# A RetNet block and a SiLU block on one core: the k and q scalings on VectorE instead of GpSimd, and the masks ahead of x and the state

## The chip, the cores and the metric

The kernel runs on one core of a Trainium2 chip. A core has TensorE (PE in the profile; PEld is its loading of weights), VectorE (DVE), ScalarE (ACT), GpSimd (POOL) and SyncE (SP), which here only issues transfers. Each engine takes its own instructions in order, and waits for others through semaphores. The metric is the device time of one execution in microseconds (us).

## The reference

Two blocks follow each other. The first is a recurrent linear attention with a decay for each of the 8 heads, over 4 batches, 768 positions and a head width of 64. The second is a pair of products with a SiLU gate between them, 512 to 2048 to 512, over the 3072 tokens of the first.

```python
for t in range(S):
    state = gamma[None, :, None, None] * state + np.einsum('bhd,bhe->bhde', k[:, :, t], v[:, :, t])
    y[:, :, t] = scale * np.einsum('bhd,bhde->bhe', q[:, :, t], state)
...
h = x @ w_in
g = h * (1.0 / (1.0 + np.exp(-h)))
return (g @ w_out).astype(np.float32)
```

x is y with heads and batches laid out as tokens.

## The kernel before

**Units and visits.** The 768 positions are cut into 6 chunks of 128. A unit is one chunk of one batch, so there are 24, in the order chunk 0 of batches 0 to 3, chunk 1 of batches 0 to 3, and so on. `visit()` (L356) number m works on three units at once: `stage_t(m)` (L274) transposes k and q of unit m on TensorE, and ScalarE copies them out of PSUM; `stage_y(m-2)` (L299) makes the new part of the state (L309) and the output y from the old state (L318) and from the masked scores (L323); `stage_a(m-1)` (L284) makes the scores of unit m-1 (L290), and VectorE multiplies them by the decay mask (L296, "am"). After that the next k, q and v are asked for, and `scale_k(m-1)` and `scale_q(m-1)` run on GpSimd (L266, L272): k is multiplied by one number per position and head, and the transposed q by one per position. Both are done in place. They follow the transposition and the scores, which need the unscaled values; the scaled ones are used by L309 and L318 in the next visit. k is not scaled in the last chunk and q not in the first, so there are 20 scalings of each. When a unit of batch 0 comes, `next_chunk()` (L248) first moves the factors of q (gq) on by one chunk, also on GpSimd (L249).

**x and the state.** Within `stage_y`, y goes from its PSUM bank into x, as three parts that TensorE can multiply: ScalarE writes the first (L339), VectorE the second from y and the first (L340) and the third from the second (L341). The new part of the state is added to the old on VectorE (L335), or copied by ScalarE in chunk 0 (L333). For chunk 2 (`LATE`), y goes to DRAM (L328, L329) and is split later.

**Banks.** One visit asks for six PSUM banks of a pool of four: k transposed, q transposed, the new part of the state, y, and the two halves of the scores. A bank is free again when what is in it has been read: by ScalarE for the transposes, by L335 (or L333) for the state, by L339 and L340 for y, by L296 for the scores.

**The first product.** `product_in(c, f)` (L376) is 12 matmuls over 128x512 (L383 to L385) for one of 16 columns of w_in, with two PSUM results, and ScalarE, VectorE and ScalarE after it (L387, L388, L389). `take_w()` (L186) brings the next piece of the weights to float32 and cuts it into three parts: six VectorE instructions in `convert_w` (L168 to L180) and, for w_in, two more in `split_w` (L105, L108), with ScalarE steps between them (L166, L103, L107).

**Order.** Visits 0 to 5 run back to back, with takes after visits 0, 1, 3 and 4. Then come the first half of the columns of chunk 0, with a visit after most single products and a take beside nearly all; the first half of chunk 1 with three visits; then the second halves of both without visits. From chunk 2 on there is a visit after every fourth product and, until the last chunk, a take at every third. Then the second product runs for all chunks (L502 to L504). TensorE's order is as written. On every other engine a planner sets the order when the kernel is built: it goes by the order of the program and by when, by its own reckoning, an instruction can start.

Of the kernel before, what the change touches and what calls it, by code (L numbers as in the profile page):

```python
# [16 lines left out]
ALU = mybir.AluOpType  # L17
# [14 lines left out]
def kernel(  # L32
# [24 lines left out]
    nc = tc.nc  # L57
# [3 lines left out]
    NC = S // C  # L61
# [51 lines left out]
    units = [(c, b) for c in range(NC) for b in range(B)]  # L113
    kqv = {"k": {}, "q": {}, "v": {}}

    def load(name, n):
        if n >= len(units):
            return
        c, b = units[n]
        src = {"k": k, "q": q, "v": v}[name]  # L120
        t = ld.tile([128, H, D], FP32, tag=f"{name}f", name=f"{name}f_{n}",
                    bufs=4 if name == "k" else 2)
        nc.sync.dma_start(out=t, in_=src[b, :, ds(c * C, C)].rearrange("h t d -> t h d"))
        kqv[name][n] = t
# [98 lines left out]
    gq = const.tile([128, HP, C], FP32, tag="gq", name="gq")  # L223
# [24 lines left out]
    def next_chunk():  # L248
        nc.gpsimd.tensor_tensor(out=gq, in0=gq,  # L249
                                in1=step[:, :HP].unsqueeze(2).to_broadcast([128, HP, C]),  # L250
                                op=ALU.mult)
# [2 lines left out]
             for b in range(B)]  # L254


    xt, kt, qt, am = {}, {}, {}, {}

    def bank(name):
        return ps_a.tile([128, 512], FP32, tag="a", name=name)  # L260

    def scale_k(n):
        if 0 <= n < len(units) and units[n][0] < NC - 1:
            t = kqv["k"][n]
            g = gk[:, units[n][0], :].unsqueeze(2).to_broadcast([128, H, D])
            nc.gpsimd.tensor_tensor(out=t, in0=t, in1=g, op=ALU.mult)  # L266

    def scale_q(n):
        if 0 <= n < len(units) and units[n][0] > 0:
            if units[n][1] == 0:  # L270
                next_chunk()
            nc.gpsimd.tensor_tensor(out=qt[n], in0=qt[n], in1=gq, op=ALU.mult)  # L272

    def stage_t(n):  # L274

        for name, src, to, bufs in (("k", kqv["k"][n], kt, 2), ("q", kqv["q"].pop(n), qt, 3)):
            tp = bank(f"{name}tp_{n}").rearrange("p (a t) -> p a t", a=HP)
            for a in range(HP):
                nc.tensor.transpose(tp[:, a, :], src[:, 2 * a : 2 * a + 2, :], ident)  # L279
            t = one.tile([128, HP, C], FP32, tag=f"{name}t", name=f"{name}t_{n}", bufs=bufs)  # L280
            evac[:] = [nc.scalar.copy(out=t, in_=tp).ins]
            to[n] = t

    def stage_a(n):  # L284

        ap = [bank(f"sc{j}_{n}").rearrange("p (a t) -> p a t", a=HP) for j in range(2)]
        ktn = kt.pop(n)
        for a in range(HP):
            for j in range(2):
                nc.tensor.matmul(ap[j][:, a, :], lhsT=ktn[ts(j, D), a, :],  # L290
                                 rhs=qt[n][ts(j, D), a, :], start=True, stop=True,
                                 skip_group_check=True)
        am[n] = []
        for j in range(2):
            t = one.tile([128, HP, C], FP32, tag=f"am{j}", name=f"am{j}_{n}")
            nc.vector.tensor_tensor(out=t, in0=ap[j], in1=decay[:, j], op=ALU.mult)  # L296
            am[n].append(t)

    def stage_y(n):  # L299

        c, b = units[n]
        kf, vs = kqv["k"].pop(n), kqv["v"].pop(n)
        qtn, amn = qt.pop(n), am.pop(n)
        if c < NC - 1:
            sp = bank(f"s_{n}")[:, : HP * D].rearrange("p (a e) -> p a e", a=HP)
            for a in range(HP):
                for j in range(2):
                    h = 2 * a + j
                    nc.tensor.matmul(sp[ts(j, D), a, :], lhsT=kf[:, h, :], rhs=vs[:, h, :],  # L309
                                     start=True, stop=True, skip_group_check=True)  # L310
        if b == 0 and c != LATE:
            xt[c] = xpool.tile([128, 3, KIN, NT], FP32R, tag="xt", name=f"xt_{c}")
        yp = bank(f"y_{n}").rearrange("p (a t) -> p a t", a=HP)

        if c > 0:
            for a in range(HP):
                for j in range(2):
                    nc.tensor.matmul(yp[ts(j, D), a, :], lhsT=state[b][ts(j, D), a, :],  # L318
                                     rhs=qtn[ts(j, D), a, :], start=(a == 0), stop=False,
                                     skip_group_check=True)  # L320
        for a in range(HP):
            for j in range(2):
                nc.tensor.matmul(yp[ts(j, D), a, :], lhsT=vs[:, 2 * a + j, :],  # L323
                                 rhs=amn[j][:, a, :], start=(c == 0 and a == 0), stop=True,
                                 skip_group_check=True)
        if c == LATE:
            y = hpool.tile([128, KIN, C], FP32, tag="hs", name=f"ys_{b}")
            nc.scalar.copy(out=y, in_=yp)  # L328
            nc.sync.dma_start(out=y_dram[b], in_=y)  # L329
        else:  # L330
            split_x(c, b, yp)
        if c == 0:
            nc.scalar.copy(out=state[b], in_=sp)  # L333
        elif c < NC - 1:
            nc.vector.tensor_tensor(out=state[b], in0=state[b], in1=sp, op=ALU.add)  # L335

    def split_x(c, b, y):
        xh, xl, xm = (xt[c][:, i, :, ts(b, C)] for i in range(3))
        nc.scalar.activation(out=xh, in_=y, func=AF.Copy, scale=HALF)  # L339
        nc.vector.tensor_tensor(out=xl, in0=y, in1=xh.bitcast(FP32), op=ALU.subtract)  # L340
        nc.vector.scalar_tensor_tensor(out=xm, in0=xl.bitcast(FP32), scalar=-1.0 / EPS,  # L341
                                       in1=xh.bitcast(FP32), op0=ALU.mult, op1=ALU.add)
# [13 lines left out]
    def visit():  # L356
        m = visits[0]
        visits[0] += 1
        if m - 2 >= len(units):
            return  # L360
        if m < len(units):
            stage_t(m)
        if m >= 2:
            stage_y(m - 2)
        if 1 <= m <= len(units):
            stage_a(m - 1)
        load("k", m + 2)
        load("q", m + 2)
        load("v", m)
        scale_k(m - 1)  # L370
        scale_q(m - 1)


    pending = []
# [64 lines left out]

    ctx.enter_context(tc.manual_schedule(engines={mybir.EngineType.PE}))  # L440
    take_w(visit)
    chunk_decays()
    for m in range(1, B + 2):
        visit()
        if m in (1, 3, 4):
            take_w()
        if m == 2:
            first_chunk()
# [5 lines left out]
    for c, f0, at, takes in phases:  # L454
        for i in range(half):
            product_in(c, f0 + i)
            if i in takes:
                take_w()
            put_g(1)
            if i in at:  # L460
                visit()
            if (c, f0) == (1, half) and 1 <= i <= B:
                late_x(i - 1)
# [22 lines left out]
    for c in range(NC):  # L486
# [7 lines left out]
        for f in range(NF):  # L494
            n = c * NF + f
            split(n + S_AHEAD)
            t = ready.pop(n)
# [44 lines left out]
```

## Time and profile before

| | before |
|---|---|
| median of 3 runs | 679.35 us (679.28 to 680.01) |
| the profiled execution | 680.86 us |
| its span in the profile | 679.1 us |
| TensorE busy | 646.3 us |
| VectorE busy | 432.0 us, 680 instructions |
| ScalarE busy | 282.0 us |
| GpSimd busy | 60.1 us, 84 instructions |

The span runs from the first to the last instruction in the profile; the time of the execution has 1.76 us around it. A busy share is an average over stages that have different limits: the stages before 150 us, with the visits and takes close together, and the long rest have to be read apart. An instruction's duration holds the time that it was kept from running on its engine; the idle time before it is shown beside it, with what ended it.

### The profile page before, as it was taken

The page shows a single profiled execution, that of the slowest core. Times are in us where ns is not written, and L with a number is a line of the kernel's source. Part 1 is how long each engine was busy: PE and PEld are TensorE (multiplying, and loading weights), DVE is VectorE, ACT ScalarE, POOL GpSimd, SP SyncE. Part 2 cuts the span into 40 slices and gives each one's busy share as a digit, 9 for nine tenths or more (in the row PEclk, how much of TensorE's full clock was granted, in tenths as well). Part 3 has the DMA queues.
Part 4 walks back from the last instruction along what each step waited for, and adds up shares of the span by engine and source line. Part 5 has one row for each costly group of instructions (what it writes and reads, how often), then busy time and mean ns, then how long its engine had stood idle before and what let it go on. Part 6 is the DMA issues. An engine that isn't in the chain of part 4 may idle for free.

```text
span 679.1 us, 10363 instructions
## 1 busy us (share of the span) xinstructions
PE 646.3 (95%) x3904; PEld 529.7 (78%) x3904; DVE 432.0 (64%) x680; ACT 282.0 (42%) x510; POOL 60.1 (9%) x84
## 2 busy tenths in 40 slices
PE   5778889999999999999999999999999999999997
PEld 3567777767888888878888888888888888888885
DVE  4899999995557675867444876545455463644641
ACT  6455466454544454443435885122222232321311
POOL 5123312300011211011000000000000000000000
PEclk9889999999999999999999999999999999999999
DMA  9958767766456665766322774424253252523401
GB/s 223 204 104 194 177 174 216 203 214 217 140 169 178 189 208 164 218 195 202 110 77 93 224 202 150 125 96 153 82 167 95 98 175 67 174 78 121 145 11 63
DMA packets 122546, 103.45 MB, mean 152 GB/s; under 512 B 79488, under 2 KB 87680, under 8 KB 122496
## 3 DMA queue, kind: packets, MB, share of 16 engines
q1 hardware_dynamic: 119040, 96.49, 50.1%
q10 hardware_dynamic: 3456, 6.29, 2.5%
q8 instruction: 31, 0.51, 0.3%
q14 instruction: 19, 0.16, 0.1%
HBM read 66.06 MB, written 36.70 MB: 151 GB/s over the span
## 4 chain that ended last, share of the span: by engine, by line
PE 82%; DVE 11%; DMA 2%; ACT 2%; issue 1%; SPq 1%; DVEq 0%; ACTq 0%
PE oa L503 13%; PE ob L504 13%; PE oa L502 13%; PE ha L383 11%; PE hb L385 11%; PE ha L384 11%; PE y L323 3%; PE sc L290 2%; PE y L318 2%; DVE wi L108 1%; DVE am L296 1%; PE qtp L279 1%; PE s L309 1%; DVE cs L173 1%; DVE wil L105 1%; DVE cs L180 1%
## 5 line engine op out<-in xcount | busy, mean ns | idle before, releaser
L385 PE MATMUL hb<-xt,wi 128*128 128x512 f32 x384 | 150.5, 392 | 4.9 <-DVE g L388 3.1
L383 PE MATMUL ha<-xt,wi 128*128 128x512 f32 x384 | 152.1, 396 | 0.0
L384 PE MATMUL ha<-xt,wi 128*128 128x512 f32 x384 | 149.8, 390 | 0.0
L504 PE MATMUL ob<-wo,gs 128*128 128x512 f32 x384 | 149.6, 390 | 0.0
L502 PE MATMUL oa<-wo,gs 128*128 128x512 f32 x384 | 149.4, 389 | 0.0
L503 PE MATMUL oa<-wo,gs 128*128 128x512 f32 x384 | 149.4, 389 | 0.0
L430 DVE TENSOR_TENSOR gs<-gr,gs 128x512 fp32r<-128x512 f32 x96 | 62.4, 685 | 92.6 <-ACT gs L428 92.6
L428 ACT ACTIVATE gs<-gr 128x512 fp32r<-128x512 f32 x96 | 53.4, 620 | 140.2 <-issue 129.7
L388 DVE TENSOR_TENSOR g<-g,hb 128x512 f32<-128x512 f32 x96 | 65.6, 684 | 69.4 <-ACT g L387 68.8
L385 PEld LDWEIGHTS hb<-xt,wi 128*128 128x128 f32 x384 | 72.1, 188 | 23.1 <-DVE g L388 6.1
L389 ACT ACTIVATE g<-g 128x512 f32<-128x512 f32 x96 | 60.6, 631 | 61.6 <-DVE g L388 61.6
L383 PEld LDWEIGHTS ha<-xt,wi 128*128 128x128 f32 x384 | 72.1, 188 | 17.4 <-ACT g L387 0.7
L504 PEld LDWEIGHTS ob<-wo,gs 128*128 128x128 f32 x384 | 72.1, 188 | 15.9 <-DVE o L510 1.1
L503 PEld LDWEIGHTS oa<-wo,gs 128*128 128x128 f32 x384 | 72.1, 188 | 15.0
L502 PEld LDWEIGHTS oa<-wo,gs 128*128 128x128 f32 x384 | 72.1, 188 | 14.9 <-ACT o L509 0.2
L384 PEld LDWEIGHTS ha<-xt,wi 128*128 128x128 f32 x384 | 72.1, 188 | 14.5 <-DVE xt L340 0.2
L387 ACT ACTIVATE g<-ha 128x512 f32<-128x512 f32 x96 | 56.7, 591 | 59.5 <-PE ha L384 54.8
L431 DVE SCALAR_TENSOR_TENSOR gs<-gs 128x512 fp32r<-128x512 f32 x96 | 62.3, 684 | 0.4
L510 DVE TENSOR_TENSOR o<-o,ob 128x512 f32<-128x512 f32 x24 | 15.9, 686 | 39.2 <-ACT o L509 39.2
L272 POOL TENSOR_TENSOR qt<-qt,gq 128x512 f32<-128x512 f32 x20 | 27.4, 1369 | 128.4 <-PE sc L290 96.2
L509 ACT ACTIVATE o<-oa 128x512 f32<-128x512 f32 x24 | 13.7, 597 | 56.7 <-PE oa L503 49.1
L266 POOL TENSOR_TENSOR kf<-kf,gk 128x512 f32<-128x512 f32 x20 | 22.7, 1134 | 154.4 <-PE ktp L279 146.2
(59 smaller groups left out, 606.8 us busy)
## 6 DMA issues: line engine op xcount, KB each, us to landing
gd<-g SPq DMA_DIRECT2D x96, 256.0 KB, 3.0
gr<-gd SPq DMA_DIRECT2D x96, 256.0 KB, 2.7
wf<-in_moe_w_in_dram SPq DMA_DIRECT2D x16, 512.0 KB, 4.2
wf<-in_moe_w_out_dram SPq DMA_DIRECT2D x16, 512.0 KB, 3.5
kf<-in_k_dram SPq DMA_DIRECT2D x24, 256.0 KB, 4.6
qf<-in_q_dram SPq DMA_DIRECT2D x24, 256.0 KB, 4.8
vf<-in_v_dram SPq DMA_DIRECT2D x24, 256.0 KB, 4.2
out_dram<-o ACTq DMA_DIRECT2D x24, 256.0 KB, 2.1
```

Of the source, the lines that this page charges most:

```text
L383: nc.tensor.matmul(ha, lhsT=w[0], rhs=x[0], start=first_, stop=False)
L384: nc.tensor.matmul(ha, lhsT=w[1], rhs=x[1], start=False, stop=last)
L385: nc.tensor.matmul(hb, lhsT=w[2], rhs=x[2], start=first_, stop=last)
L387: nc.scalar.activation(out=hs, in_=ha, func=AF.Copy, scale=ONE_E)
L388: nc.vector.tensor_tensor(out=hs, in0=hs, in1=hb, op=ALU.subtract)
L389: nc.scalar.activation(out=hs, in_=hs, func=AF.Silu)
L428: nc.scalar.activation(out=t[:, 0, :], in_=g, func=AF.Copy, scale=HALF)
L430: nc.vector.tensor_tensor(out=t[:, 1, :], in0=g, in1=high, op=ALU.subtract)
L431: nc.vector.scalar_tensor_tensor(out=t[:, 2, :], in0=t[:, 1, :].bitcast(FP32), scalar=-1.0 / EPS, in1=high, op0=ALU.mult, op1=ALU.add)
L502: nc.tensor.matmul(oa, lhsT=gh, rhs=wo[f][:, 0, :], start=first_, stop=False)
L503: nc.tensor.matmul(oa, lhsT=glo, rhs=wo[f][:, 1, :], start=False, stop=last)
L504: nc.tensor.matmul(ob, lhsT=gm, rhs=wo[f][:, 2, :], start=first_, stop=last)
```

## The change

Both scalings are issued on VectorE. `next_chunk()` stays on GpSimd. The part of `stage_y` that follows its matmuls (y into x, the state) becomes `finish_y`, which keeps the two PSUM tiles in `live` until it runs. In a visit the scalings now stand right behind `stage_a`, q before k, and `finish_y(m-2)` behind them; the three loads come last. The matmuls keep their order, and the store of y in `finish_y` still stands ahead of the visit's loads.

```diff
     def scale_k(n):
         if 0 <= n < len(units) and units[n][0] < NC - 1:
             t = kqv["k"][n]
             g = gk[:, units[n][0], :].unsqueeze(2).to_broadcast([128, H, D])
-            nc.gpsimd.tensor_tensor(out=t, in0=t, in1=g, op=ALU.mult)
+            nc.vector.tensor_tensor(out=t, in0=t, in1=g, op=ALU.mult)
...
             if units[n][1] == 0:
                 next_chunk()
-            nc.gpsimd.tensor_tensor(out=qt[n], in0=qt[n], in1=gq, op=ALU.mult)
+            nc.vector.tensor_tensor(out=qt[n], in0=qt[n], in1=gq, op=ALU.mult)
...
+        live[n] = sp if c < NC - 1 else None, yp
+
+    def finish_y(n):
+        c, b = units[n]
+        sp, yp = live.pop(n)
         if c == LATE:
...
             stage_y(m - 2)
         if 1 <= m <= len(units):
             stage_a(m - 1)
+            scale_q(m - 1)
+            scale_k(m - 1)
+        if m >= 2:
+            finish_y(m - 2)
         load("k", m + 2)
         load("q", m + 2)
         load("v", m)
-        scale_k(m - 1)
-        scale_q(m - 1)
```

More of the change, by code (lines that the diff above doesn't have):

```diff
@@ L254 @@
              for b in range(B)]
-    xt, kt, qt, am = {}, {}, {}, {}
+    xt, kt, qt, am, live = {}, {}, {}, {}, {}
     def bank(name):
```

## The prediction

> **What bounds the kernel now.** I read the page first, then the busy times by stage, then who waits for whom in the early stages, then single rows.
>
> ```profile
> span 679.1 us, 10363 instructions
> PE 646.3 (95%) x3904; PEld 529.7 (78%) x3904; DVE 432.0 (64%) x680; ACT 282.0 (42%) x510; POOL 60.1 (9%) x84
> ...
> 14.00:41.00 27.00, 19.52 (x221) 15.84 (x221) 23.90 (x36) 12.47 (x26) 5.71 (x6) 0.87 0.86 168
> 41.00:85.00 44.00, 37.73 (x376) 30.89 (x373) 42.97 (x65) 21.43 (x38) 13.36 (x10) 1.00 0.75 174
> 85.00:147.00 62.00, 56.93 (x439) 45.58 (x438) 59.72 (x98) 35.20 (x63) 11.44 (x9) 1.00 0.73 197
> 147.00:360.00 213.00, 211.96 (x1443) 174.20 (x1442) 131.62 (x205) 97.25 (x168) 23.25 (x19) 1.00 0.55 173
> ```
>
> The last four rows are stages: limits, length, then busy time of PE, PEld, DVE, ACT and POOL, the granted clock, the DMA share and GB/s. Over the whole span TensorE is the bound. From 147 us on it is idle for 213.00 - 211.96 = 1.04 us up to 360, where the last scaling has run: nothing that VectorE saves or loses there shows, as long as it is not late. From 14 to 147 us it is otherwise. VectorE is busy 42.97 of 44 and 59.72 of 62 us, which is 102.7 of 106, and 23.90 of 27 before that; TensorE has 7.48 + 6.27 + 5.07 = 18.8 us idle there. Only these can be won. The waits of the first stage (two rows) and of 41 to 147 us (three rows) say for whom it waits:
>
> ```profile
> PE qtp L279 <- DVE xt L340: 4.7, 2, 2.3
> PE y L323 <- DVE am L296: 1.1, 2, 0.9
> ...
> PE s L309 <- DVE am L296: 4.5, 2, 2.5
> PE hb L385 <- DVE g L388: 2.1, 3, 1.0
> PE hb L385 <- DVE xt L341: 1.8, 1, 1.8
> ```
>
> All are VectorE: its backlog sets how fast TensorE gets through this part, and the end comes when TensorE has done what is left. So the question is what the change does to VectorE's work before 147 us.
>
> **What it removes.** One scaling of k beside VectorE's instructions, in order of time:
>
> ```profile
> 28.18 0.68 DVE L177 SCALAR_TENSOR_TENSOR cp<-wf,cp 128x512 f32<-128x512 uint32 x1
> 28.66 1.11 POOL L266 TENSOR_TENSOR kf<-kf,gk 128x512 f32<-128x512 f32 x1 [6.33 <-PE ktp L279]
> 28.78 1.53 DVE L341 SCALAR_TENSOR_TENSOR xt<-xt 128x512 fp32r<-128x512 f32 x1
> 30.24 1.28 DVE L296 TENSOR_TENSOR am<-sc,decay 128x512 f32<-128x512 f32 x2
> ```
>
> GpSimd begins at 28.66 us and ends at 29.77. L341, begun behind it, takes 1.53 us; an instruction of its kind and size beside it takes 0.68. It looks as if L341 does its work once GpSimd has ended. By the Trainium skill, "SBUF — State Buffer", section "Who interferes with whom", a VectorE instruction with two SBUF inputs, or one in a two-port mode, and a GpSimd instruction that reads SBUF exclude each other for a whole instruction; the two rows agree, and by that rule the whole lengthening goes. How often it happens, from VectorE's groups in 41 to 147 us (seven rows) and in 137 to 160 us, where GpSimd does nothing (four rows):
>
> ```profile
> L108 DVE SCALAR_TENSOR_TENSOR wi<-wi,wil 128x512 fp32r<-128x512 f32 x13 | 12.3, 942 | 0.2
> L173 DVE SCALAR_TENSOR_TENSOR cs<-ca,cs 128x512 uint32<-128x512 uint32 x14 | 12.0, 861 | 0.3
> L105 DVE SCALAR_TENSOR_TENSOR wil<-cs,wi 128x512 f32<-128x512 f32 x13 | 10.4, 801 | 1.9 <-ACT wi L103 1.5
> L180 DVE TENSOR_TENSOR cs<-cs,cp 128x512 f32<-128x512 f32 x12 | 10.0, 831 | 0.1
> L170 DVE TENSOR_SCALAR ca<-ca 128x512 f32<-128x512 f32 x13 | 9.3, 717 | 0.0
> L175 DVE TENSOR_SCALAR cp<-cs 128x512 uint32<-128x512 uint32 x14 | 7.1, 509 | 0.2
> L341 DVE SCALAR_TENSOR_TENSOR xt<-xt 128x512 fp32r<-128x512 f32 x5 | 4.5, 893 | 0.0
> ...
> L173 DVE SCALAR_TENSOR_TENSOR cs<-ca,cs 128x512 uint32<-128x512 uint32 x4 | 2.8, 692 | 0.1
> L180 DVE TENSOR_TENSOR cw<-cs,cp 128x512 f32<-128x512 f32 x4 | 2.8, 692 | 0.3 <-DMA wod<-cw 0.2
> L170 DVE TENSOR_SCALAR ca<-ca 128x512 f32<-128x512 f32 x4 | 1.7, 423 | 1.0 <-ACT ca L166 1.0
> L175 DVE TENSOR_SCALAR cp<-cs 128x512 uint32<-128x512 uint32 x4 | 1.7, 423 | 0.1
> ```
>
> Against 692 ns for the two-tensor forms and 423 for L170 and L175, the excess is 13 x 0.250 (L108) + 14 x 0.169 (L173) + 13 x 0.109 (L105) + 12 x 0.139 (L180) + 13 x 0.294 (L170) + 14 x 0.086 (L175) + 5 x 0.201 (L341) = 14.7 us. In 14 to 41 us, three groups are long by the same measure:
>
> ```profile
> L173 DVE SCALAR_TENSOR_TENSOR cs<-ca,cs 128x512 uint32<-128x512 uint32 x3 | 3.5, 1172 | 0.1
> L341 DVE SCALAR_TENSOR_TENSOR xt<-xt 128x512 fp32r<-128x512 f32 x3 | 2.9, 960 | 0.0
> L168 DVE TENSOR_SCALAR cs<-wf 128x512 uint32<-128x512 uint32 x2 | 1.7, 841 | 0.0
> ```
>
> 3 x 0.480 + 3 x 0.268 + 2 x 0.418 = 3.1 us. Who makes it, from GpSimd's groups in 14 to 147 us and one of its gq steps beside L180:
>
> ```profile
> L266 POOL TENSOR_TENSOR kf<-kf,gk 128x512 f32<-128x512 f32 x12 | 14.2, 1179 | 48.1 <-PE ktp L279 39.9 <-issue 8.2
> L272 POOL TENSOR_TENSOR qt<-qt,gq 128x512 f32<-128x512 f32 x9 | 13.1, 1458 | 40.3 <-PE sc L290 31.4 <-ACT wi L103 6.2 <-ACT xt L339 2.7
> L249 POOL TENSOR_TENSOR gq<-gq,step 128x512 f32<-128x512 f32 x3 | 3.2, 1083 | 0.8 <-ACT gq L246 0.6
> ...
> 122.10 1.10 POOL L249 TENSOR_TENSOR gq<-gq,step 128x512 f32<-128x512 f32 x1
> ...
> 122.23 1.52 DVE L180 TENSOR_TENSOR cs<-cs,cp 128x512 f32<-128x512 f32 x1
> ```
>
> Twelve scalings of k (four before 41 us) and nine of q go; the three gq steps stay, and one of them costs L180 1.52 - 0.69 = 0.83 us. For the three I leave 1.1 us in place (bounds: nothing, or 3 x 0.83 = 2.5). Removed: 14.7 + 3.1 - 1.1 = 16.7 us, or 0.80 for each of 21.
>
> **What it adds.** 21 VectorE instructions of 128x512 with three f32 operands in SBUF, as L180 is (692 ns). What one takes from VectorE is the step to the next instruction:
>
> ```profile
> 41.08 0.69 DVE L340 TENSOR_TENSOR xt<-y,xt 128x512 fp32r<-128x512 f32 x1 [0.55 <-ACT xt L339]
> 41.69 0.68 DVE L105 SCALAR_TENSOR_TENSOR wil<-cs,wi 128x512 f32<-128x512 f32 x1
> 41.70 1.79 POOL L272 TENSOR_TENSOR qt<-qt,gq 128x512 f32<-128x512 f32 x1 [6.24 <-ACT wi L103]
> 42.29 1.75 DVE L341 SCALAR_TENSOR_TENSOR xt<-xt 128x512 fp32r<-128x512 f32 x1
> ...
> 44.09 0.50 PE L385 MATMUL hb<-xt,wi 128*128 128x512 f32 x1 [1.77 <-DVE xt L341]
> ```
>
> 41.08 to 41.69 to 42.29: 0.60 us each. The trace has no VectorE instruction whose input is broadcast as gk is; its step is bounded by 0.42 (the whole of a one-tensor L170 undisturbed) and 0.73 (0.69 and a small gap). I take 0.60, the nearest row: 21 x 0.60 = 12.6 us, between 8.8 and 15.3.
>
> **The sum.** Before 41 us four scalings: 4 x 0.60 - 3.1 = -0.7. From 41 to 147 us seventeen: 17 x 0.60 = 10.2, less 14.7 - 1.1 = 13.6, so -3.4. Together -4.1 us of VectorE's work, between -7.9 and -1.4 with the bounds of the added step. VectorE has next to no idle time there, so I pass it on whole. The profiled execution was 680.86 us for a span of 679.1: it would become 676.8, its span 675.0. It lies 1.5 us over the median of 679.35, from which I get 675.25, rounded to **675.2 us**.
>
> **Moves costed at nothing.** The scalings issue no transfer; y's store (L329) and the loads keep their order on SP's queue. In 147 to 360 us the added steps lie beside a TensorE that has its inputs ready. The masks now come before L340 and L341: x is up to four steps (2.4 us) later, but VectorE does the same work, and a stall of 0.7 to 0.9 us per scaling is gone. A scaling of q for batch 0 waits for gq on GpSimd, and behind it in VectorE's queue stand the scaling of k, x, the state and the next take. GpSimd has nothing else to do and can start gq once the last scaling of the chunk before is done, a whole visit ahead. If it did not, each of five would cost 1.1 us, and only two fall into 41 to 147 us: 2.2.
>
> **Rivals.**
> *The order pays too* (chance 0.15). The masks free two score banks first, and the two transposes of the next visit can go there instead of waiting for L340 (4.7 us), and L309 no longer for L296 (4.5). While VectorE is the bound, this can win only its idle time, 27 - 23.90 + 106 - 102.7 = 6.4 us. All of it gives 668.8; I put the case at half, 672.0. Against it: VectorE's idle time is partly waits for ScalarE inside a take.
> *The saving is not passed on* (0.14). TensorE is itself busy 94.7 of 106 us. If VectorE's free time turns into waits for TensorE or ScalarE, half of it or less arrives at the end: 677.3 to 679.4, which I put at 678.6.
> *The banks of y and of the state are held longer* (0.11): slower. They are now freed behind two masks and two scalings. TensorE waits for them if its next visit asks for a third bank before VectorE is through, and between visits 6 to 10 it has one product of 12 matmuls, at 0.23 us each 2.8, to cover four steps of 0.60 and L340, 3.0. If every visit up to 85 us lost its scalings, that is 4 x 0.60 in chunk 0 and 5 x 1.20 after it, 8.4 us, and the first product, which already waits 1.77 us for L341 at 44.09, would lose 2.4 more. With the saving: 675.2 + 10.8 = 686.0; with only half of the visits hit, 680.6. I put it at 683. For it: TensorE's waits for L340. Against it: the rows at 41.08 and 41.69, where VectorE takes L340 before the masks because it is ready first; the planner may do so again.
> *The lengthening has another cause, and VectorE just gets more work* (0.03): 679.35 + 12.6 = 692.0. The Trainium skill, "Perfetto Trace Analysis", section "Optimizing Scalar/DVE Operations", says that with a saturated VectorE some work may go to GpSimd, which speaks against this change; it adds that the two share a port, so that it might not help. Against the rival: L341 above, and that VectorE's long rows lie beside GpSimd's.
> That the planner puts the scalings or x elsewhere than written is part of the forecast, since the sum doesn't hang on the order.
>
> **How the numbers follow.** The forecast has 0.57, with its own range from 671.4 (-7.9) to 677.9 (-1.4). A measurement can tell about 0.2%, 1.4 us: faster is below 678.0. Faster: 0.57 + 0.15 = 0.72; same: 0.14; slower: 0.11 + 0.03 = 0.14. The range of 8 in 10 reaches down to 670.5, into the first rival, and up to 681.0, over the second and the lower part of the third.
>
> **What would show it.** Right: VectorE's long rows are at 692 and 423 ns in 41 to 147 us but for those beside L249; L266 and L272 on VectorE at about 0.69 us; VectorE's busy time about as before (it counts 0.69 for a step of 0.60); TensorE's idle time in 14 to 147 us near 14.7 us instead of 18.8. Wrong: scalings at 1 us and more, long rows that stay, waits of L309 or L323 for L340, L333 or L335 that add up to over 4 us, or any new idle time of TensorE after 147 us.

## The result and the profile after

| | before | after |
|---|---|---|
| median of 4 runs on one chip | 679.68 us (679.28 to 680.19) | 663.60 us (662.50 to 663.89) |
| ratio, 95% interval | | 0.976 (0.9743 to 0.9777) |
| the profiled execution and its span | 680.86, 679.1 us | 663.32, 661.2 us |

The kernel is 16.1 us faster. The forecast was 675.2 us with a range from 670.5 to 681.0: the direction is right, the gain is about four times as large, and the time lies outside the range.

The first two lines of the page of after, and its busy times by stage in the columns of before (PE, PEld, DVE, ACT, POOL, clock, DMA share, GB/s):

```profile
span 661.2 us, 10308 instructions
PE 639.6 (97%) x3904; PEld 525.1 (79%) x3904; DVE 424.1 (64%) x720; ACT 285.2 (43%) x510; POOL 11.1 (2%) x44
```

```profile
14.00:41.00 27.00, 20.38 (x250) 16.10 (x250) 25.75 (x46) 14.47 (x29) 1.04 (x1) 1.00 0.91 181
41.00:85.00 44.00, 43.42 (x440) 35.86 (x439) 44.00 (x85) 26.86 (x46) 1.36 (x1) 1.00 0.90 214
85.00:147.00 62.00, 61.47 (x424) 50.66 (x423) 58.28 (x108) 38.36 (x68) 1.04 (x1) 1.00 0.72 210
147.00:360.00 213.00, 212.15 (x1464) 173.64 (x1463) 131.88 (x224) 100.52 (x173) 2.71 (x2) 1.00 0.56 170
```

TensorE's idle time between 41 and 147 us fell from 6.27 + 5.07 = 11.3 us to 0.58 + 0.53 = 1.1. Before 41 us it is still idle for 6.6 of 27. VectorE issues more than before (85 and 108 rows instead of 65 and 98) in about the same busy time. Over the span TensorE's idle time went from 679.1 - 646.3 = 32.8 to 661.2 - 639.6 = 21.6 us, and its busy time fell by 6.7 for the same 3904 matmuls: together the 17.9 us of the span.

VectorE's groups between 14 and 147 us (x count, busy us, mean ns; L346 is the old L341, L345 the old L340, L395 the old L388):

```profile
L173 DVE SCALAR_TENSOR_TENSOR cs<-ca,cs 128x512 uint32<-128x512 uint32 x19 | 13.1, 688 | 0.2
...
L105 DVE SCALAR_TENSOR_TENSOR wil<-cs,wi 128x512 f32<-128x512 f32 x15 | 10.9, 726 | 2.4 <-ACT wi L103 2.1
L108 DVE SCALAR_TENSOR_TENSOR wi<-wi,wil 128x512 fp32r<-128x512 f32 x15 | 10.3, 689 | 0.1
L180 DVE TENSOR_TENSOR cs<-cs,cp 128x512 f32<-128x512 f32 x15 | 10.3, 687 | 0.0
L170 DVE TENSOR_SCALAR ca<-ca 128x512 f32<-128x512 f32 x19 | 8.4, 440 | 1.8 <-ACT ca L166 1.8
L266 DVE TENSOR_TENSOR kf<-kf,gk 128x512 f32<-128x512 f32 x12 | 8.2, 687 | 0.0
...
L272 DVE TENSOR_TENSOR qt<-qt,gq 128x512 f32<-128x512 f32 x9 | 6.2, 689 | 0.0
L346 DVE SCALAR_TENSOR_TENSOR xt<-xt 128x512 fp32r<-128x512 f32 x8 | 5.5, 688 | 0.0
```

The long rows of before (942 ns for L108, 861 for L173, 717 for L170) are at 689, 688 and 440. The 21 scalings take 687 to 689, whether their second input is broadcast (gk) or not. The largest of what is left of TensorE's waits for VectorE in the same stretch:

```profile
PE qtp L279 <- DVE xt L345: 3.2, 3, 1.5
...
PE s L309 <- DVE am L296: 1.1, 2, 0.5
PE hb L392 <- DVE g L395: 0.8, 2, 0.5
```

So each single cost was as forecast, and still the gain is four times the forecast sum. That is the question for the experiments: why 12.6 us of added work did not show in the time.

### The profile page after: what moved, and what is told of

It is laid out like the page before. It is cut to its first block, busy times and chain, and to the rows that moved or that the text cites. A ratio compares the mean times of both kernels' runs of the same rounds, so it can differ in the third digit from the quotient of the medians.

```text
span 661.2 us, 10308 instructions
## 1 busy us (share of the span) xinstructions
PE 639.6 (97%) x3904; PEld 525.1 (79%) x3904; DVE 424.1 (64%) x720; ACT 285.2 (43%) x510; POOL 11.1 (2%) x44
## 4 chain that ended last, share of the span: by engine, by line
PE 78%; DVE 14%; DMA 4%; issue 2%; ACT 1%; SPq 0%; DVEq 0%; ACTq 0%
PE ob L511 13%; PE oa L510 13%; PE oa L509 13%; PE ha L390 10%; PE hb L392 10%; PE ha L391 10%; PE y L323 2%; PE y L318 2%; PE sc L290 2%; DVE am L296 2%; DVE g L395 2%; DVE cp L177 1%; DVE wil L105 1%; DVE cs L173 1%; DMA vf<-in_v_dram 1%
## 5 line engine op out<-in xcount | busy, mean ns | idle before, releaser
L435 ACT ACTIVATE gs<-gr 128x512 fp32r<-128x512 f32 x96 | 53.5, 622 | 140.0 <-issue 129.6
L395 DVE TENSOR_TENSOR g<-g,hb 128x512 f32<-128x512 f32 x96 | 65.8, 685 | 67.0 <-ACT g L394 67.0
L390 PEld LDWEIGHTS ha<-xt,wi 128*128 128x128 f32 x384 | 72.0, 188 | 18.8 <-ACT g L394 2.1
L394 ACT ACTIVATE g<-ha 128x512 f32<-128x512 f32 x96 | 57.1, 595 | 66.9 <-PE ha L391 62.0
L391 PEld LDWEIGHTS ha<-xt,wi 128*128 128x128 f32 x384 | 72.1, 188 | 14.7 <-DVE xt L345 0.4
L296 DVE TENSOR_TENSOR am<-sc,decay 128x512 f32<-128x512 f32 x48 | 31.5, 685 | 1.6 <-PE sc L290 1.6
L290 PE MATMUL sc<-qt,kt 64*128 64x128 f32 x384 | 28.6, 290 | 0.0
```

Source lines behind the costliest of these rows:

```text
L390: nc.tensor.matmul(ha, lhsT=w[0], rhs=x[0], start=first_, stop=False)
L391: nc.tensor.matmul(ha, lhsT=w[1], rhs=x[1], start=False, stop=last)
L394: nc.scalar.activation(out=hs, in_=ha, func=AF.Copy, scale=ONE_E)
L395: nc.vector.tensor_tensor(out=hs, in0=hs, in1=hb, op=ALU.subtract)
L435: nc.scalar.activation(out=t[:, 0, :], in_=g, func=AF.Copy, scale=HALF)
```

## The experiments

Progress is told by the time at which TensorE starts the last matmul (L385) of a numbered product. The 17th product is the first of the second halves (chunk 0, column 8); that time is 141.2 us before and 123.0 after.

**e1_engine: the engine alone.** The kernel before, with only this:

```diff
-            nc.gpsimd.tensor_tensor(out=t, in0=t, in1=g, op=ALU.mult)
+            nc.vector.tensor_tensor(out=t, in0=t, in1=g, op=ALU.mult)
...
-            nc.gpsimd.tensor_tensor(out=qt[n], in0=qt[n], in1=gq, op=ALU.mult)
+            nc.vector.tensor_tensor(out=qt[n], in0=qt[n], in1=gq, op=ALU.mult)
```

> The kernel before with both scalings on VectorE and nothing moved. Theory A (order): what won is that VectorE serves TensorE's masks first, so this keeps only the 4 us of work that the sum gave: 675 us, TensorE idle in 14 to 147 us still some 15 us. Theory B (engine): the lengthened VectorE instructions sat on the chain that TensorE waits for, and TensorE's clock fell in the waits; with them gone most of the 16 us is here: 664 to 668 us, granted clock 1.00 in 22 to 42 us.

**e2_order: the order alone.** The kernel after, with the same two lines back on `nc.gpsimd`.

> The changed kernel with both scalings back on GpSimd: the new order alone. Theory A: 666 to 669 us, that is 11 to 14 us of the 16, with VectorE's long instructions still there. Theory B: within 2 us of the kernel before (678 to 681), TensorE's waits for VectorE and the low clock remain.

**e3_none_old: neither lengthening nor added work.** The kernel before without the two lines, so that the scalings are left out and VectorE has the same instructions as before.

> The kernel before without the 40 scalings of k and q (left out; y and all after it come out without the decay between chunks). No lengthening and no added work, in the old order. Theory A: the old order still makes TensorE wait: 670 us or more. Theory B: as fast as the changed kernel or faster, 658 to 664 us.

**e4_scal_last: the scalings behind x and the state.** The kernel after, with `finish_y` ahead of the scalings.

```diff
             stage_a(m - 1)
-            scale_q(m - 1)
-            scale_k(m - 1)
         if m >= 2:
             finish_y(m - 2)
+        scale_q(m - 1)
+        scale_k(m - 1)
         load("k", m + 2)
```

> The changed kernel with the scalings behind x and the state: masks, x, state, scalings, all on VectorE. If the place of the scalings matters less than the masks ahead of x, this is within 2 us of the changed kernel (662 to 666). If x and the state had to come behind the scalings, it lies halfway to the engine-only kernel.

Measured in one batch, where the kernel before had 680.11 us:

| | us | ratio, 95% | product 17 at |
|---|---|---|---|
| e1, engine alone | 663.55 | 0.9759 (0.9744 to 0.9775) | 127.1 |
| e2, order alone | 680.43 | 1.0008 (0.9996 to 1.0019) | 144.5 |
| e3, no scalings | 665.39 | 0.9785 (0.9770 to 0.9800) | 127.2 |
| e4, scalings last | 664.92 | 0.9775 (0.9760 to 0.9789) | 126.7 |

The engine is the whole gain, and the order brings nothing: e2 is the time of before, and e1 and e4 cannot be told from after by their intervals. Theory B of the expectations (the engine) holds against theory A (the order), though e3 is 1.4 us slower than B allowed. e3 is the telling one. Its VectorE runs the same 680 instructions as before in the same order, and nothing is added; yet it is no faster than e1, which carries all the scalings. Two rows at the 17th subtraction (L388; L386 in e3, which is two lines shorter), from VectorE's timeline of before and then of e3:

```profile
143.46 0.69 DVE L180 TENSOR_TENSOR cw<-cs,cp 128x512 f32<-128x512 f32 x1
144.07 0.68 DVE L388 TENSOR_TENSOR g<-g,hb 128x512 f32<-128x512 f32 x1
```

```profile
128.98 0.69 DVE L180 TENSOR_TENSOR cw<-cs,cp 128x512 f32<-128x512 f32 x1
129.59 0.68 DVE L386 TENSOR_TENSOR g<-g,hb 128x512 f32<-128x512 f32 x1
```

The same neighbours, 14.5 us earlier. In e3 TensorE is busy from 41 us on nearly as in after:

```profile
14.00:41.00 27.00, 19.62 (x229) 15.59 (x227) 23.91 (x37) 13.11 (x27) 5.98 (x5) 0.87 0.83 168
41.00:85.00 44.00, 43.19 (x441) 35.56 (x442) 42.38 (x79) 26.82 (x46) 0.00 (x0) 1.00 0.87 206
85.00:147.00 62.00, 61.49 (x420) 50.10 (x419) 56.20 (x103) 37.34 (x66) 0.00 (x0) 1.00 0.79 235
```

The first row also settles a side question: e3 has the granted clock of before in that stage (0.87; after has 1.00) and nearly the whole gain, so the clock of that stage isn't what made the difference.

To see where the scalings' time went in e1 and after, I counted VectorE's rows up to the start of the 17th subtraction: idle and lengthened time from 14 us on, take rows and scalings from the start. "Lengthened" is what rows take over 0.69 us (two tensors) or 0.42 (one tensor, or the state):

| | reached at | idle | lengthened | take rows (L105 to L180) | scalings |
|---|---|---|---|---|---|
| before | 144.1 | 6.3 | 18.4 | 135 | 0 |
| e3 | 129.6 | 7.1 | 3.0 | 135 | 0 |
| e1 | 128.6 | 4.4 | 1.2 | 123 | 23 |
| after | 125.5 | 2.6 | 0.8 | 122 | 23 |

From before to e3 the lengthening falls by 15.4 and the point is reached 14.5 earlier: passed on nearly whole. From e3 to e1, the 21 scalings that come after 14 us add 12.6, and the point comes 1.0 *earlier*. In the rows: 12 take instructions fewer stand ahead (at about 0.50 each, the mean of three steps of 0.33 and five of 0.60, 6.0 us), idle time is 2.7 less, and lengthening 1.8 less. That leaves 1.0 + 12.6 - 6.0 - 2.7 - 1.8 = 3.1, and closer steps make up for it: without idle and lengthened time, a row with two tensors takes 0.621 us on average in e3 (136 rows) and 0.608 in e1 (150), the others 0.374 (56) and 0.347 (51), which is 150 x 0.013 + 51 x 0.027 = 3.3. In before, L180 follows L177, on which it depends, after 0.72 us (142.74 to 143.46). In after other work stands between:

```profile
43.73 0.69 DVE L266 TENSOR_TENSOR kf<-kf,gk 128x512 f32<-128x512 f32 x1
44.33 0.42 DVE L175 TENSOR_SCALAR cp<-cs 128x512 uint32<-128x512 uint32 x1
44.69 0.69 DVE L296 TENSOR_TENSOR am<-sc,decay 128x512 f32<-128x512 f32 x1
45.30 0.68 DVE L177 SCALAR_TENSOR_TENSOR cp<-wf,cp 128x512 f32<-128x512 uint32 x1
45.90 0.68 DVE L296 TENSOR_TENSOR am<-sc,decay 128x512 f32<-128x512 f32 x1
46.50 0.68 DVE L180 TENSOR_TENSOR cs<-cs,cp 128x512 f32<-128x512 f32 x1
```

e3 is not free of a stall of its own, though. Nothing holds back the gq steps there, and all five run at once, ahead of the first product; beside them four rows of VectorE take 1.15 to 1.41 us, which is most of its 3.0 us of lengthening. TensorE's longest wait of e3 in 14 to 147 us lies there, 1.3 us in before and absent in e1:

```profile
14.73 6.29 POOL L249 TENSOR_TENSOR gq<-gq,step 128x512 f32<-128x512 f32 x5 [2.45 <-ACT gq L246]
```

```profile
PE ktp L277 <- ACT state L331: 3.4, 1, 3.4
```

TensorE starts the first matmul that needs the third part of x (L385 and its like) at 44.09 us in before, 42.68 in e3, 38.79 in e1 and 37.46 in after. So e1 is 3.9 us ahead of e3 there and level with it at the 17th product. In between, with 17 of the scalings (10.2 us), e1 takes 88.3 us and e3 84.5. The added work is therefore not free: about 3.8 us of it is paid in that stretch, and a lead won before the first product hides it. How much of that lead is e3's own stall and how much is e1's new plan (ScalarE copies the state at 17.23 us in e1, ahead of a take step, and at 22.14 in e3, behind it) no run separates.

The theory from here on: the planner knows of work that an instruction brings, and puts it into holes and ahead of takes that nobody needs yet; it knows nothing of the lengthening, which falls on whatever stands there. The rival: VectorE simply had room for 12.6 us. The next four test both sides.

**e5_takes_first: the takes held where they were.** e1, with each mask (L296) and each subtraction (L388) of the first stages held behind as many take instructions as in before.

```diff
+            with behind("am"):
+                nc.vector.tensor_tensor(out=t, in0=ap[j], in1=decay[:, j], op=ALU.mult)
...
+        with behind("g"):
+            nc.vector.tensor_tensor(out=hs, in0=hs, in1=hb, op=ALU.subtract)
```

> The engine-only kernel, with VectorE's masks (L296) and subtractions (L388) of the first stage held behind as many instructions of the takes as in the kernel before. Its VectorE does the same work without lengthening. Theory P (the planner): the 12.6 us of added steps cost nothing only because the planner let takes slip behind what TensorE waits for; with the old places the time rises to 669 to 676 us. Theory F (VectorE has room): it stays at 663 to 666 us.

**e6_double: the added work once more.** After, with a second VectorE instruction behind each scaling, of the same size (the maximum of the tile with itself).

```diff
             nc.vector.tensor_tensor(out=t, in0=t, in1=g, op=ALU.mult)
+            nc.vector.tensor_tensor(out=t, in0=t, in1=t, op=ALU.max)
```

> The changed kernel with a second VectorE instruction behind each scaling, the maximum of the tile with itself, in place: 40 more of the same size, 21 of them before the takes of w_in are through (21 x 0.60 to 0.73 = 12.6 to 15.3 us of VectorE). Theory P: the planner lets more takes slip, 664 to 668 us. Theory W (each us of VectorE's work before 147 us costs one, as the prediction had it): 676 to 679 us.

**e7_write_only: GpSimd writes and doesn't read.** Before, with a fill in place of each scaling.

```diff
-            nc.gpsimd.tensor_tensor(out=t, in0=t, in1=g, op=ALU.mult)
+            nc.gpsimd.memset(t, 1.0)
```

> The kernel before with each scaling on GpSimd replaced by a fill of the same tile with 1.0, which writes it and reads nothing (the scalings are left out, what follows uses the ones). VectorE's order is that of the kernel before. If GpSimd's reads are what lengthens VectorE's two-tensor instructions, these stay at 0.69 us and the time is near that of the kernel without scalings, 665 to 669 us; one-tensor instructions (L168, L170, L175) may still be long. If any GpSimd instruction beside VectorE does it, the time stays above 672 us.

**e8_stall_and_work: the added work with the lengthening.** Before, with a VectorE maximum of the tile with itself ahead of each GpSimd scaling.

```diff
+            nc.vector.tensor_tensor(out=t, in0=t, in1=t, op=ALU.max)
             nc.gpsimd.tensor_tensor(out=t, in0=t, in1=g, op=ALU.mult)
```

> The kernel before, scalings on GpSimd, with one VectorE instruction ahead of each: the maximum of the tile with itself, in place. So both the lengthening and the added VectorE work are there. Theory P: the added work is planned and slides, the lengthening is not: 678 to 684 us, the kernel before or a little more. Theory W: 680 + 12.6 = 692 us or more.

The batch, with 679.77 us for the kernel before:

| | us | ratio, 95% | product 17 at |
|---|---|---|---|
| e5, takes held in front | 677.07 | 0.9958 (0.9942 to 0.9975) | 140.6 |
| e6, work twice | 673.39 | 0.9904 (0.9875 to 0.9934) | 136.9 |
| e7, GpSimd only writes | 666.28 | 0.9798 (0.9781 to 0.9815) | 128.2 |
| e8, work and lengthening | 678.98 | 0.9986 (0.9975 to 0.9997) | 139.7 |

*e7* confirms the removed part by itself. VectorE's groups of e7 between 14 and 147 us, and GpSimd's:

```profile
L108 DVE SCALAR_TENSOR_TENSOR wi<-wi,wil 128x512 fp32r<-128x512 f32 x15 | 10.3, 689 | 0.3
L105 DVE SCALAR_TENSOR_TENSOR wil<-cs,wi 128x512 f32<-128x512 f32 x15 | 10.3, 689 | 3.4 <-ACT wi L103 3.0
...
L341 DVE SCALAR_TENSOR_TENSOR xt<-xt 128x512 fp32r<-128x512 f32 x8 | 5.5, 685 | 0.0
```

```profile
L266 POOL MEMSET kf<- 128x512 f32 x12 | 7.5, 624 | 52.0 <-PE ktp L279 52.0
...
L272 POOL MEMSET qt<- 128x512 f32 x9 | 4.9, 540 | 35.7 <-PE sc L290 35.7
```

GpSimd is at work on the same tiles at the same places and VectorE's rows with two tensors are short; the time is that of e3 within 0.9 us. It is GpSimd's reading that lengthens them. The gq steps, which read, stay in e7 and run before 22 us: there VectorE's rows beside them take 0.96 to 1.41 us. One-tensor rows aren't quite spared by fills: between 41 and 147 us, L168 takes 0.79 at 69.28 us and L170 0.70 at 116.18, instead of 0.42. The Trainium skill, "SBUF — State Buffer", section "Who interferes with whom", says that a VectorE instruction with two SBUF inputs contends with a GpSimd instruction that reads SBUF and not with one that only writes it; by that rule, the trace agrees (689 ns beside the fills, 942 for L108 in the kernel before).

*e5* takes most of the gain back: 13.5 us over e1, with the lengthening gone and the same instructions, and 1.1 us more than theory P expected at most. Two of its stages, and TensorE's largest wait in 41 to 147 us (L397 is the old L385, L401 the old L388):

```profile
41.00:85.00 44.00, 40.01 (x425) 32.64 (x424) 42.41 (x77) 24.15 (x42) 1.36 (x1) 1.00 0.79 191
85.00:147.00 62.00, 54.20 (x370) 43.78 (x370) 55.04 (x100) 34.36 (x59) 1.09 (x1) 0.92 0.65 191
```

```profile
PE hb L397 <- DVE g L401: 7.5, 2, 3.8
```

So the same instructions in another order cost 13.5 us more. It isn't a pure test of the takes, and that 677.07 lies near the forecast of 675.2 proves nothing. By the same count its 17th subtraction is reached at 141.5, 12.9 behind e1, with 10 take rows more (5.0 us) but also with 5.8 us more of idle VectorE, which comes with the fixed order.

*e6* missed both expectations: it lies between theory P's 664 to 668 and theory W's 676 to 679. The second portion of 21 instructions, 12.6 to 15.3 us by the prediction's bounds, costs 9.8 over after (673.39 - 663.60), so most of it is paid. Only two take rows more give way (120 instead of 122 ahead of the 17th subtraction). In this plan little room is left after one portion. As for the rival, idle time alone was never room for 12.6 us: e3 has 7.1 up to the 17th subtraction. TensorE's largest waits are for VectorE (L394 the old L385, L348 x, L397 the subtraction; 0.4 and 0.8 us in after):

```profile
PE hb L394 <- DVE xt L348: 3.1, 1, 3.1
PE hb L394 <- DVE g L397: 2.7, 2, 2.0
```

*e8* is not a clean corner of the square. Its time is that of before, but its lengthening up to the 17th subtraction is 13.6 instead of 18.4, and a wait appears that before doesn't have, since GpSimd's scaling now follows an instruction of VectorE (L320 makes y from q, L274 scales it):

```profile
PE y L320 <- POOL qt L274: 8.5, 5, 2.3
```

So it shows no price of the work by itself.

**e9_gq: gq on VectorE too.** After, to take the last of the lengthening away.

```diff
-        nc.gpsimd.tensor_tensor(out=gq, in0=gq,
+        nc.vector.tensor_tensor(out=gq, in0=gq,
```

> The changed kernel with the five gq steps on VectorE too, so that GpSimd does nothing beside VectorE after 20 us. Three steps before 147 us: up to 0.83 us of lengthening each goes, 3 x 0.60 comes, and scalings of q for batch 0 no longer wait for another engine. If lengthening alone costs: 661 to 663 us. If it is all the same to VectorE: 663 to 665 us.

**e10_takes_later** and **e11_before_takes_later: fewer takes in front by hand.** The places of the takes in the first stages are moved back, in after and in before.

```diff
-    phases = ((0, 0, (0, 1, 2, 3, 5), (0, 1, 2, 3, 4, 5, 6)),
-              (1, 0, (1, 3, 5), (0, 1, 2, 3, 5)),
-              (0, half, (), (2, 6)),
-              (1, half, (), (7,)))
+    phases = ((0, 0, (0, 1, 2, 3, 5), (0, 1, 3, 5)),
+              (1, 0, (1, 3, 5), (1, 3, 5, 7)),
+              (0, half, (), (0, 1, 2, 3)),
+              (1, half, (), (2, 6)))
```

> The changed kernel with eight takes of w_in in place of twelve beside the first sixteen products, and four beside the next four, just ahead of the columns that need them. Theory P (VectorE's load costs TensorE time only through takes that stand in front of what TensorE waits for and that nobody needs yet): TensorE idle in 41 to 147 us stays under 1.5 us, and the time is 660 to 664 us, since there is little idle time left to win. If VectorE's total before the last take is what counts: no change, 663 to 665.

> The kernel before, scalings on GpSimd, with the same later takes. VectorE's lengthening stays. Theory P: with fewer takes in front most of the lengthening finds room, 664 to 671 us, TensorE idle in 41 to 147 us 2 to 5 us instead of 11.3. If the lengthening hits TensorE's chain whatever stands in front (the scalings' neighbours are masks and x): 676 to 680 us.

**e12_before_takes_mid: the same in before, with the last pieces of w_in earlier than in e11.** In the places of the takes three go from the first phase, and the second and the fourth get one each, so that there is one fewer in all.

```diff
-    phases = ((0, 0, (0, 1, 2, 3, 5), (0, 1, 2, 3, 4, 5, 6)),
-              (1, 0, (1, 3, 5), (0, 1, 2, 3, 5)),
-              (0, half, (), (2, 6)),
-              (1, half, (), (7,)))
+    phases = ((0, 0, (0, 1, 2, 3, 5), (0, 1, 3, 5)),
+              (1, 0, (1, 3, 5), (0, 1, 2, 3, 5, 7)),
+              (0, half, (), (0, 2)),
+              (1, half, (), (2, 6)))
```

> The kernel before, scalings on GpSimd, with the takes beside the first products spread so that the last two pieces of w_in come in good time (two take places fewer in the first phase, one more in the second, none lost in all). Ahead of the 17th subtraction L388 stand 119 take instructions instead of 135. Theory (the takes that stand in front of what TensorE waits for cost the kernel before as much as the lengthening does, and any 12 to 16 instructions of VectorE that leave that place are worth 7 to 9 us): the 17th product ends 7 to 10 us earlier than before (131 to 134 us instead of 141.2), no product after it waits over 1 us for w, and the time is 670 to 674. Rival (only GpSimd's scalings cost time; the takes are needed soon after, and what they give up in front comes back as waits for the weights): 678 to 681, with waits of L383 to L385 for w or of the second product later in the trace.

The kernel before had 680.36 us beside the first three and 680.01 beside e12:

| | us | ratio, 95% | product 17 at |
|---|---|---|---|
| e9, gq on VectorE | 667.04 | 0.9806 (0.9782 to 0.9830) | 129.4 |
| e10, after, takes later | 664.73 | 0.9775 (0.9750 to 0.9801) | 122.4 |
| e11, before, takes later | 679.96 | 0.9987 (0.9969 to 1.0005) | 130.8 |
| e12, before, takes in between | 678.00 | 0.9966 (0.9951 to 0.9981) | 137.5 |

None of the four beats after. e9 was a miss, 667.04 against 661 to 665, although the stalls that GpSimd's gq steps make are gone; three of its five added steps lie before 147 us, 1.8 us of work, and it costs 3.4. The trace shows one place for it. For the first product VectorE does the third part of x (L346) 0.9 us behind the second (L345) in after, and 3.9 us behind it in e9, where two more take rows, both masks and a scaling of q stand between. After, then e9, then TensorE's wait in e9:

```profile
35.78 0.69 DVE L345 TENSOR_TENSOR xt<-y,xt 128x512 fp32r<-128x512 f32 x1
...
36.71 0.69 DVE L346 SCALAR_TENSOR_TENSOR xt<-xt 128x512 fp32r<-128x512 f32 x1
```

```profile
37.10 0.68 DVE L345 TENSOR_TENSOR xt<-y,xt 128x512 fp32r<-128x512 f32 x1
...
41.03 0.69 DVE L346 SCALAR_TENSOR_TENSOR xt<-xt 128x512 fp32r<-128x512 f32 x1
```

```profile
41.78 0.50 PE L392 MATMUL hb<-xt,wi 128*128 128x512 f32 x1 [3.44 <-DVE xt L346]
```

In after that matmul starts at 37.46, 4.3 us earlier, and waits 0.43. So the place of one row in the plan can be worth as much as all that e9 lost. e6 has the same row late as well: its matmul starts at 42.22, 4.8 us behind after, where the 17th product is 13.9 behind. Why the planner chose so, no run shows.

e10 ends level with after, near what both theories allowed. With 103 take rows ahead of the 17th subtraction instead of 122 the 17th product comes only 0.6 us sooner, and TensorE's idle time in 41 to 147 us is 3.4 us, where theory P had under 1.5.

e11 and e12 were to give the kernel before part of the gain without touching the scalings, and both missed at the end: 679.96 is in the rival's range of e11, and 678.00 at the lower edge of the rival's in e12. The 17th product did come sooner, by 10.4 and 3.7 us (the theory of e12 had 7 to 10 there), and e11's TensorE idle time in 41 to 147 us fell to 3.6 us as theory P had it. In e11 the last pieces of w_in were then late. TensorE's longest waits from 147 to 200 us:

```profile
PE ha L383 <- ACT wi L103: 2.5, 1, 2.5
PE ha L384 <- ACT wi L107: 1.8, 2, 0.9
```

In e12 no product waited for the weights, and the 13th product was 5.9 us ahead (116.8 instead of 122.7) and the 15th only 2.5. The timeline between them:

```profile
123.22 0.63 ACT L103 ACTIVATE wi<-cs 128x512 fp32r<-128x512 f32 x1 [4.04 <-DVE cs L180]
...
125.62 0.58 ACT L281 COPY kt<-ktp 128x512 f32<-128x512 f32 x1
...
126.25 2.37 PE L290 MATMUL sc<-qt,kt 64*128 64x128 f32 x16 [2.83 <-ACT kt L281]
```

ScalarE waits 4.04 us for VectorE's L180 in a take step (L103), and the copy of the transposed k (L281), whose input was there since about 120.3 us, stands behind it in its queue; TensorE waits 2.83 us for that copy. So a take can hold TensorE up through ScalarE's queue as well, and fewer takes by hand is a different plan, with its own holes. e11 and e12 therefore don't confirm that the deferred takes alone pay for the scalings. Nor do they price the takes' place up to the 17th product: with fewer takes ahead of the 17th subtraction (103 and 119), the lengthening ahead of it was less too (9.8 and 15.5 us instead of 18.4), and VectorE was idle for longer (18.9 and 11.2 us instead of 6.3).

## Why the prediction was wrong in size

- **What bounds the kernel: right.** VectorE's backlog held TensorE up between 14 and 147 us, though not alone: 41 to 147 us also had 2.9 us of waits for ScalarE's copies (L281, ahead of the scores), which the prediction's rows leave out. With the backlog lowered, TensorE's idle time there is 7.7 us; the forecast said 14.7, before was 18.8.
- **What it removes, 16.7 us: right.** The long rows went to 688 and 440 ns, e7 names GpSimd's reads as the cause, and e3 has 14.7 us less than before (680.11 - 665.39). That it is passed on to the end nearly whole was right too; the rival "not passed on" falls.
- **What it adds, 21 steps of 0.60: right as a row, wrong as a cost.** VectorE does spend it (43.73 to 44.33 above). But e1, with the work, takes 663.55 us and e3, without it, 665.39; in the stretch where the two can be set side by side, from the first to the 17th product, 3.8 of 10.2 us was paid.
- **The sum is the step that failed:** "Together -4.1 us of VectorE's work ... so I pass it on whole". It netted planned work against unplanned stalls one for one, as if every microsecond of VectorE before 147 us stood in front of TensorE. The forecast had -0.7 us before 41 us and -3.4 from there to 147. Up to the first product e1 won 5.3 us and after 6.6; from there to the 17th product they won 8.8 and 11.6. VectorE's queue there held some 130 take instructions, part of which was not needed yet. A stall is paid at the place where it falls, since the order was fixed when the kernel was built. New instructions are planned: 12 or 13 take rows moved behind the 17th subtraction, idle time shrank by 1.9 to 3.7 us, and neighbours closed up. In the prediction's own words VectorE had "next to no idle time", and that was taken for "nothing can move"; it also held that "the sum doesn't hang on the order", and e5, with e1's instructions in another order, is 13.5 us slower. Without the added 12.6 the same working gives 679.35 - 16.7 = 662.7, 0.9 us from the result. That it is so near is partly luck: some of the added work was paid, and a better plan before the first product made up for it.
- **The order as written, costed at nothing: right.** It brings nothing with the scalings on GpSimd (e2: 1.0008) nor with them on VectorE (after 663.60, e1 663.55). The rivals "the order pays too" and "the banks are held longer" fall with that. Nor was gq late: among TensorE's waits of after in 14 to 147 us there is none for the scaled q (L272).
- **After 147 us: right** (TensorE 212.15 of 213). Part of the lead over before was lost again there: 20.0 us at the 22nd product (136.6 against 156.6) and 16.5 at the 32nd (167.3 against 183.8), with TensorE waiting for VectorE's subtraction and for ScalarE's step ahead of it (0.5 and 0.8 us from 140 to 170). That the deferred takes came due there is likely, but not shown.

Shown are the lengthening, its cause and that it is passed on (e3, e7), and that most of the added work was not paid (e1 against e3) while most of a second portion is (e6). How the unpaid part divides between later takes, idle time, closer steps and a better plan before the first product is read from the rows of single executions. e5 and e9 show that the place of rows in VectorE's order is worth microseconds, but e5 brings idle time of its own, and e11 and e12 could not isolate the takes. That the planner's choice explains all of it stays a theory.

## What to carry to other kernels

Price a stall and an added instruction differently when the order of an engine is fixed ahead: here the stall fell on whatever stood there and went nearly straight through, while the instruction was placed, and cost little as long as work that wasn't due yet could give way. So before netting the two, ask which instructions on the busy engine have a late due date; and where an instruction on one engine lengthens another's, count what it costs there (here about 0.80 us of VectorE for each scaling on GpSimd, against 0.60 done by VectorE itself). A new plan can also move one row that TensorE waits for by some 4 us (e9), so a difference of that size between two plans says little about the work itself.

## What was not expected of the hardware

- By the profile, whose spans on GpSimd are rough, its fill of 128x512 took 0.53 to 0.82 us between 41 and 110 us of e7, beside rows of VectorE with two tensors that stayed at 0.69; its multiplication of the same size takes 1.18 (k) and 1.46 us (q) on average in before, and costs VectorE up to 1.11 us at a time (L170 at 69.25 us, 1.53 instead of 0.42).
- A wait of TensorE can cost more than its length, when the granted clock (the number behind the brackets) falls behind it. The wait of 2.83 us in e12 ends at 126.25 (behind the wait of 1.77 us in before, which ends at 44.09, the clock stayed at 1.00):

```profile
122.00:126.00 4.00, 1.42 (x24) 1.01 (x20) 3.72 (x7) 2.62 (x5) 0.00 (x0) 1.00 0.59 176
126.00:128.00 2.00, 1.75 (x15) 1.56 (x15) 0.98 (x3) 2.00 (x5) 0.00 (x0) 0.74 1.09 228
128.00:130.00 2.00, 2.00 (x7) 1.49 (x6) 1.93 (x3) 0.91 (x2) 1.20 (x1) 0.50 1.04 243
130.00:132.00 2.00, 2.00 (x9) 1.65 (x8) 1.97 (x5) 0.00 (x0) 0.09 (x1) 0.91 0.93 266
```

The first matmuls of the next product take 0.79, 0.63, 0.63 and 0.58 us, where those a little later take 0.39. By the Trainium skill, "TensorE: Matmul & The Clock Gate", section "What's actually happening", the clock is halved after an idle window of about 3.4 us and restored after a busy one; the rows agree with the half clock, here after a wait shorter than that. Of the 17.9 us that the span lost from before to after, 6.7 are a shorter busy time of the same matmuls. In e1, as fast in the runs, that is only 2.9 (643.4 us busy), so most of this share isn't needed for the gain.
